# Moving two kinds of low-part subtraction from VectorE, which read PSUM, to GpSimd, which reads an SBUF copy made by ScalarE

## The chip, the cores and the metric

The kernel runs on one core of a Trainium2 chip. The metric is the device time of one execution in microseconds. Engines are named as in the profile: PE is TensorE (matmuls; PEld its weight loads), DVE is VectorE, ACT is ScalarE, POOL is GpSimd, SP is the engine whose queue issues most of the DMAs.

## The reference, cut to what matters

Attention that keeps the 32 largest scores of each row, then a feed-forward layer with a gated activation, then a layer of eight experts of which each token uses one. All inputs are float32.

```python
scores = scale * np.matmul(q, k.transpose(0, 1, 3, 2))   # 4 batches, 8 heads, 576 rows, 64 wide
kth = np.partition(scores, -32, axis=-1)[..., -32:-31]
scores = np.where(scores >= kth, scores, -1e9)
...
x = np.matmul(softmax(scores), v)                         # heads joined: 2304 tokens x 512
h = x @ w_in                                              # 512 -> 2048
g = h * np.clip(h + 3.0, 0.0, 6.0) / 6.0
x = g @ w_out                                             # 2048 -> 512
...
ye = np.maximum(x[mask] @ w1[e], 0.0) @ w2[e]             # 8 experts, mask = tokens of expert e
out[mask] = gate_w[mask, None] * ye
```

## The kernel before, in words

**High and low parts.** TensorE multiplies in a rounded float32 format here. An operand is therefore kept as a rounded part (h) and the remainder that rounding dropped (l), and a product is built from two or three matmuls. A remainder is made by a subtraction: unrounded value minus rounded value. For the transposed queries the parts are `qh` and `ql`, for the transposed attention output `xh` and `xl`.

**Tiles and visits.** The 576 query rows of a batch are cut where blocks of 256 tokens end, so parts are 64, 128, 192 or 256 rows wide. A visit (48 in all, numbered n) is one part of one pair of heads. A visit holds one tile per head and 128 rows, and for the last 64 rows one tile "T" that stacks both heads: 144 tiles t in all. At a change of batch the visits of the old and the new batch alternate, and visits 64 rows wide hold one tile only.

**The loop over tiles.** Step t of the main loop puts work of several tiles side by side: the score matmuls of tile t+2 (`qk`, L585, into `sps`), their copy to SBUF by ACT (`sevac`, into `sbuf`), the search for the largest scores on DVE (`top_a`: L615, L621, L626; `top_z`: L648; `mask`: L675, L679, L683), the transposes of the probabilities (`trans`, L699, into `ptps`), the product with v (`pv`, L733), and one step g of the feed-forward layer (`moe_step`: L807 into `l1ps`, L819 on DVE, `gh` and `gl` on POOL, L838 into `yps`). In the first 34 steps or so each step also converts one piece of the feed-forward weights (`conv64`: L293, L300, L303 on DVE, L262 and L311 on POOL).

**Preparing queries.** `qprep(n)` transposes the rows of visit n on PE (L434, and L436 for a last 64 rows) into the single-buffer PSUM tile `misc`; ACT copies it with rounding to `qh` (L442, L448); DVE subtracts `qh` from the PSUM tile into `ql` (L452, L456). Both are read by the score matmuls of that visit. The raw rows come by DMA into the tile `qn` (L488, L491, on SP's queue), which has one buffer: the DMAs of visit n+1 wait until the transposes of visit n have read it. Keys are prepared alike by `kprep` (L402, L403 on POOL, L409, L417 on PE).

**Turning the attention output.** `xt` transposes the output of 128 rows and two heads on PE (L769) into `misc`; ACT copies with rounding to `xh` (L779); DVE subtracts into `xl` (L783). Both are operands of L807. It runs 80 times, 16 of them for a tile T, where both ACT and DVE work in two pieces of 64x64.

**What sets the order.** Each engine works in order. A scheduler sets that order at build time from priorities (the table `PRIO`) and its own estimate of when things are ready, so a change of one instruction can move its neighbours.

After the attention loop, from about 860 us on, the rest of the feed-forward layer and the experts follow.

Of the kernel before, what the change touches and what calls it, by code (L numbers as in the profile page):

```python
# [13 lines left out]
F32 = mybir.dt.float32  # L14
# [4 lines left out]
AF = mybir.ActivationFunctionType  # L19
ALU = mybir.AluOpType  # L20
# [36 lines left out]
def attention_two_moe_kernel(  # L57
# [13 lines left out]
    PE, V, A, G, SP = nc.tensor, nc.vector, nc.scalar, nc.gpsimd, nc.sync  # L71
# [4 lines left out]
    NE, _, F2 = w1.shape  # L76
    P = 128
# [53 lines left out]
    def r_(ap):  # L131
        return ap.bitcast(F32)
# [4 lines left out]
    def pr(name, least=0):  # L137
        tc.cur_priority = max(least, pr0[0] + PRIO[name])

    def run(gen):  # L140
        for _ in gen:
            pass
# [54 lines left out]
    def body(cs, exact):  # L197
# [12 lines left out]
        ap1 = at.enter_context(tc.tile_pool(name="ap1" + X, bufs=1, side="right"))  # L210
# [20 lines left out]
        def misc(shape):  # L231
            m = boot.pop(0) if boot else None
            if m is not None:
                return m if len(shape) == 3 else m[:, 0:shape[1]]
            misc_n[0] += 1
            return ps1.tile(shape, F32, tag="misc", bufs=1, name=f"misc{misc_n[0]}")
# [147 lines left out]
        def rows(h):  # L384
            return slice(h * D, (h + 1) * D)
# [40 lines left out]
        def qprep(n):  # L426
            b, p, q0, w, first = visits[n]
            pr(pk[0])
            qn = qraw.pop(n)
            nf = w // P  # L430
            mp = misc([P, 2, 2 * P])
            for h in range(2):
                for j in range(nf):
                    PE.transpose(mp[:, h, j * P:(j + 1) * P], qn[:, j, h, :, :].rearrange("p a d -> p (a d)"), ident)  # L434
                if w % P:
                    PE.transpose(mp[:, h, nf * P:w], qn[0:TAIL, nf, h, :, :].rearrange("p a d -> p (a d)"), ident[0:TAIL, 0:TAIL])  # L436
            yield
            pr(pk[0])
            fw = nf * P
            st = [ap1.tile([P, 2, 2 * P], F32R, tag=f"q{i}", bufs=QB, name=f"q{i}{n}") for i in "hl"]  # L440
            if nf:
                A.activation(st[0][:, :, 0:fw], mp[:, :, 0:fw], AF.Copy)  # L442
            if w % P:

                for i in st:
                    G.memset(r_(i[:, :, fw:fw + P]), 0.0)  # L446
                for h in range(2):
                    A.activation(st[0][:, h, fw + h * D:fw + (h + 1) * D], mp[:, h, fw:w], AF.Copy)  # L448
            yield
            pr(pk[0])  # L450
            if nf:
                V.tensor_tensor(st[1][:, :, 0:fw], mp[:, :, 0:fw], r_(st[0][:, :, 0:fw]), op=ALU.subtract)  # L452
            if w % P:
                for h in range(2):
                    hc = slice(fw + h * D, fw + (h + 1) * D)
                    V.tensor_tensor(st[1][:, h, hc], mp[:, h, fw:w], r_(st[0][:, h, hc]), op=ALU.subtract)  # L456
            qx[n] = st
            yield
            pr(pk[0])
# [73 lines left out]
        def pstart(tl, age=AGE):  # L533
            if pjob[0] is None:
                kind = pick(tl, age)
                if kind == "k":
                    pjob[0] = ("k", kprep(*kjobs[kdone[0]]))
                elif kind == "q":
                    pjob[0] = ("q", qprep(qdone[0]))
            return pjob[0]  # L540
# [219 lines left out]
        def xt(n, o, t):  # L760
            b, p, q0, w, first = visits[n]
            r0 = b * S + q0
            bk, off = divmod(r0, TB)
            xh, xl = xbuf[bk % 2]
            while bk >= 2 and gpos[0] < (bk - 1) * NF1:
                run(moe_step())
            mp = misc([P, P])
            pr("xt0")
            PE.transpose(mp, xp.pop((n, o)), ident)  # L769
            yield  # L770
            if o == "T":
                off += w // P * P
                parts = [(rows(h), slice(off, off + 64), rows(h)) for h in range(2)]
            else:
                off += o * P
                parts = [(slice(0, P), slice(off, off + P), slice(0, P))]
            pr("xt1")
            for r, cl, m in parts:
                A.activation(xh[r, p, cl], mp[r, m], AF.Copy)  # L779
            yield  # L780
            pr("xt2")
            for r, cl, m in parts:
                V.tensor_tensor(xl[r, p, cl], mp[r, m], r_(xh[r, p, cl]), op=ALU.subtract)  # L783
            if t == vlast[n] and p == NPAIR - 1 and (r0 + w) % TB == 0:
                blkready[0] = bk + 1

# [177 lines left out]
        def moe_step():  # L964
            g = gpos[0]
            if g >= NG + 3 or (g < NG and blkready[0] <= g // NF1):
                return
            gpos[0] += 1
            if 0 <= g - 1 < NG:
                epi_a(g - 1)  # L970
            yield
            if g >= 3:
                l2(g - 3)
                bk, f = divmod(g - 3, NF1)
                if f == NF1 - 1:
                    for tt, y in enumerate(yevac(bk)):
                        pend.append([gate(bk, tt, y), 0])
            yield
            if 0 <= g - 1 < NF1:
                conv_upto(2 * (g - 1) + 1)  # L980
            if 0 <= g - 1 < NG:
                load_wo(g - 1)
            if 0 <= g - 2 < NG:
                epi_c(g - 2)
            yield
            if 0 <= g - 1 < NG:
                epi_b(g - 1)
            yield
            if g < NG:
                if g < NF1:  # L990
                    conv_upto(2 * g)
                l1(g)
# [29 lines left out]
        for t in range(T + 7):  # L1022
# [23 lines left out]
            if xtq and (xtq[0][2] < t - 5 or t >= T):  # L1046
                xg = xt(*xtq.pop(0))
                next(xg)
# [141 lines left out]
        for s in range(len(seq) + 2):  # L1190
            if s < len(seq):
                e, f = seq[s]
# [85 lines left out]
    with tc.If(todo > 0):  # L1278
# [4 lines left out]
        for e in range(NE):  # L1283
            n = nc.values_load(ctl[0:1, 2 + e:3 + e], min_val=0, max_val=NT)
# [32 lines left out]
```

## Time and profile before

| what | value |
|---|---|
| median of 3 runs | 1261.87 us (1261.56 to 1262.14) |
| profiled execution, its own time | 1263.75 us |
| its span, first to last instruction | 1261.9 us |
| busy over the span: PE, DVE, ACT, POOL | 91%, 76%, 65%, 32% |
| mean granted TensorE clock | 0.968 |

The busy shares are averages over stages with different limits: DVE is 7 to 9 tenths busy in every slice from 32 us to about 850 us and mostly 2 to 4 tenths after that. The profiled execution took 1263.75 us, 1.88 us above the median, and 1.85 us of it lie around the span.

### The profile page before, as it was taken

Reading aid. Unit: us, or ns where it says so; the run is one execution under the profiler, and the core shown is the slowest. Engines: PE = TensorE matmul, PEld = TensorE weight load, DVE = VectorE, ACT = ScalarE, POOL = GpSimd, SP = SyncE. Lnnn points to the kernel's source line nnn. Section 1 sums busy time; section 2 is a strip of 40 time slices with the busy share of each in tenths; the row PEclk is TensorE's granted clock in tenths of the full one; section 3 lists DMA queues with packets and bytes.
Section 4 is the critical chain, followed back from the end, with each engine's and each line's share of the span. In section 5 each row is a group of like instructions: output and inputs, shape, how many; then the busy total and the mean of one; then the engine's idle time right before and its main releaser. Section 6 shows DMA issues by size and latency. Waiting matters only on the chain.

```text
span 1261.9 us, 23710 instructions
## 1 busy us (share of the span) xinstructions
PE 1146.6 (91%) x7333; PEld 1031.2 (82%) x7333; DVE 954.9 (76%) x3820; ACT 816.7 (65%) x2089; POOL 408.1 (32%) x649
## 2 busy tenths in 40 slices
PE   5476579899999999999999999999985999999995
PEld 4365467789999899999898999998875999999994
DVE  5999999999999899998997999995413444444420
ACT  4777777778888788787777887784413444444421
POOL 3542255743322443323433322223433022221100
PEclk9998689999999999999999999999986999999997
DMA  3644456555543555634435545444854455455400
GB/s 89 207 131 141 127 173 228 151 163 144 143 136 123 133 153 154 163 117 132 123 107 156 144 121 148 124 120 123 305 174 118 150 179 156 155 174 154 128 19 26
DMA packets 184664, 180.20 MB, mean 143 GB/s; under 512 B 123933, under 2 KB 148813, under 8 KB 184528
## 3 DMA queue, kind: packets, MB, share of 16 engines
q1 hardware_dynamic: 178960, 167.24, 45.5%
q0 software_dynamic: 4416, 11.08, 2.9%
q8 instruction: 60, 0.98, 0.3%
q14 instruction: 76, 0.62, 0.2%
q10 hardware_dynamic: 1152, 0.28, 0.1%
HBM read 160.52 MB, written 19.59 MB: 143 GB/s over the span
## 4 chain that ended last, share of the span: by engine, by line
PE 69%; DVE 18%; ACT 5%; DMA 4%; issue 2%; POOL 1%; SPq 0%; POOLq 0%; DVEq 0%; ACTq 0%
PE l1ps L807 12%; PE yps L838 12%; PE lp L1152 11%; PE ops L1169 10%; PE ptps L733 8%; PE sps L585 5%; PE ptps L699 4%; DVE pbuf L683 3%; DVE z L648 2%; DVE cd L615 2%; DVE z L675 2%; DVE cw L626 1%; DVE m L621 1%; PE misc L434 1%; PE misc L409 1%
## 5 line engine op out<-in xcount | busy, mean ns | idle before, releaser
L838 PE MATMUL yps<-wo,gh 128*128 128x512 f32 x576 | 217.4, 419 | 0.5 <-DMA wo<-wod 0.5
L615 DVE MAX8 cd<-sbuf 128x8 f32<-128x72 f32 x1152 | 187.2, 218 | 2.8 <-ACT sbuf L264 2.5
L262 POOL TENSOR_SCALAR gh<-gf 128x256 fp32r<-128x256 f32 x144 | 73.7, 512 | 355.4 <-PE yps L838 233.9
L807 PE MATMUL l1ps<-xh,wih 128*128 128x256 f32 x576 | 168.8, 293 | 14.3 <-DVE gf L819 7.0
L807 PE MATMUL l1ps<-xl,wih 128*128 128x256 f32 x576 | 165.2, 287 | 0.0
L807 PE MATMUL l1ps<-xh,wil 128*128 128x256 f32 x576 | 164.6, 286 | 0.0
L956 DVE TENSOR_TENSOR wl<-raw,wh 128x1024 fp32r<-128x1024 f32 x64 | 79.2, 1239 | 94.8 <-ACT wh L955 92.7
L733 PE MATMUL ptps<-vn,pt 128*128 128x65 f32 (+1 forms) x1152 | 146.5, 281 | 0.0
L733 PEld LDWEIGHTS ptps<-vn,pt 128*128 128x128 f32 x1152 | 143.5, 201 | 0.0
L683 DVE SCALAR_TENSOR_TENSOR pbuf<-sbuf,tall,pbuf 128x576 f32<-128x576 f32 x144 | 135.2, 939 | 0.1
L648 DVE SCALAR_TENSOR_TENSOR z<-sbuf,uall 128x576 f32<-128x576 f32 x144 | 131.2, 911 | 2.5 <-ACT uall L639 2.4
L807 PEld LDWEIGHTS l1ps<-xh,wih 128*128 128x128 f32 x576 | 111.0, 193 | 24.7 <-DVE gf L819 11.9
L955 ACT ACTIVATE wh<-raw 128x1024 fp32r<-128x1024 f32 x64 | 67.6, 1060 | 84.0 <-PE lp L1152 44.7
L838 PEld LDWEIGHTS yps<-wo,gh 128*128 128x128 f32 x576 | 108.0, 191 | 16.9 <-POOL qh L446 0.7
L827 POOL TENSOR_TENSOR gl<-gf,gh 128x256 fp32r<-128x256 f32 x144 | 118.1, 820 | 11.3
L838 PE MATMUL yps<-wo,gl 128*128 128x512 f32 x288 | 116.5, 405 | 0.6 <-POOL gl L827 0.6
L699 PE MATMUL ptps<-ident,pbuf 128*128 128x128 f32 x576 | 97.9, 295 | 20.0 <-DVE j L679 17.4
L807 PEld LDWEIGHTS l1ps<-xl,wih 128*128 128x128 f32 x576 | 111.4, 193 | 4.3
L665 ACT ACTIVATE jk<-sbuf,uall 128x576 bf16<-128x576 f32 x144 | 112.0, 777 | 4.3 <-DVE j L679 0.8
L264 ACT ACTIVATE sbuf<-sps 128x576 f32<-128x576 f32 x144 | 93.1, 647 | 32.3 <-PE sps L585 21.5
L656 ACT ACTIVATE pbuf<-sbuf,nb 128x576 f32<-128x576 f32 x144 | 111.3, 776 | 4.1 <-PE ptps L701 0.8
L807 PEld LDWEIGHTS l1ps<-xh,wil 128*128 128x128 f32 x576 | 111.5, 194 | 0.0
(197 smaller groups left out, 2934.5 us busy)
## 6 DMA issues: line engine op xcount, KB each, us to landing
wo<-wod SPq DMA_DIRECT2D x144, 512.0 KB, 3.8
raw<-in_moe_w_dram SPq DMA_DIRECT2D x64, 512.0 KB, 4.0
vn<-in_v_dram SPq DMA_DIRECT2D x96, 128.0 KB, 2.7
rawi<-in_moe_w_in_dram SPq DMA_DIRECT2D x16, 512.0 KB, 4.1
rawo<-in_moe_w_out_dram SPq DMA_DIRECT2D x16, 512.0 KB, 3.8
wod<-wc SPq DMA_DIRECT2D x16, 512.0 KB, 3.8
qn<-in_q_dram SPq DMA_DIRECT2D x126, 64.0 KB, 2.6
yd<-y SPq DMA_DIRECT2D x18, 258.0 KB, 4.1
```

The costliest lines, as they stand in the source:

```text
L615: V.max(cd[:, c, :], s[:, c * CK:(c + 1) * CK])
L648: V.scalar_tensor_tensor(d["z"], s, d["u"], s, op0=ALU.is_le, op1=ALU.mult)
L656: A.activation(d["p"], d["s"], AF.Exp, bias=d["nb"], scale=SCALE)
L665: A.activation(jk, d["s"][:, 0:S], AF.Sign, bias=ts[t]["u"], scale=-1.0, accum_out=d["sg"])
L683: V.scalar_tensor_tensor(d["p"], d["s"], tall[:, t:t + 1], d["p"], op0=ALU.is_ge, op1=ALU.mult)
L699: PE.transpose(ptps[:, c * P:(c + 1) * P], pb[:, c0 + c * P:c0 + (c + 1) * P], ident)
L733: PE.matmul(d_, a_, b_, start=(i == 0), stop=(i == len(mm) - 1))
L807: PE.matmul(dst, a[:, c, fs], b_[:, c, :], start=(n == 0), stop=(n == 3 * NCC - 1))
L827: G.tensor_tensor(gl, gf, r_(gh), op=ALU.subtract)
L838: PE.matmul(yps[tt], a[:, tsl], b_, start=(f == 0 and m == 0), stop=(f == NF1 - 1 and m == 2))
L1152: PE.matmul(lp, a[:, c, fs], b_[:, c, :], start=(n == 0), stop=(n == 3 * NCC - 1))
L1169: PE.matmul(ops_[j], a[:, js], b_[:, ns], start=(f == 0 and m == 0), stop=(f == NF2 - 1 and m == 2))
```

## The change

`qprep`, for every visit but the first, has ACT copy the PSUM tile a second time, unrounded, into a new SBUF tile `qr`; POOL subtracts `qh` from `qr` into `ql`. The tile `qr` uses the one buffer of the tag `qn`, the raw query rows. `xt` has ACT copy its PSUM tile unrounded into a new SBUF tile `xr` (two buffers of its own); POOL subtracts `xh` from it into `xl`.

```diff
             pr(pk[0])
+            if n == 0:
+                e_, qr = V, mp
+            else:
+                e_, qr = G, ap1.tile([P, 2, 2 * P], F32, tag="qn", bufs=1, name=f"qr{n}")
+                A.activation(qr[:, :, 0:w], mp[:, :, 0:w], AF.Copy)
             if nf:
-                V.tensor_tensor(st[1][:, :, 0:fw], mp[:, :, 0:fw], r_(st[0][:, :, 0:fw]), op=ALU.subtract)
+                e_.tensor_tensor(st[1][:, :, 0:fw], qr[:, :, 0:fw], r_(st[0][:, :, 0:fw]), op=ALU.subtract)
             if w % P:
                 for h in range(2):
                     hc = slice(fw + h * D, fw + (h + 1) * D)
-                    V.tensor_tensor(st[1][:, h, hc], mp[:, h, fw:w], r_(st[0][:, h, hc]), op=ALU.subtract)
+                    e_.tensor_tensor(st[1][:, h, hc], qr[:, h, fw:w], r_(st[0][:, h, hc]), op=ALU.subtract)
...
             for r, cl, m in parts:
                 A.activation(xh[r, p, cl], mp[r, m], AF.Copy)
+            xr = ap1.tile([P, P], F32, tag="xr", bufs=2, name=f"xr{n}_{o}")
+            A.activation(xr, mp, AF.Copy)
             yield
             pr("xt2")
             for r, cl, m in parts:
-                V.tensor_tensor(xl[r, p, cl], mp[r, m], r_(xh[r, p, cl]), op=ALU.subtract)
+                G.tensor_tensor(xl[r, p, cl], xr[r, m], r_(xh[r, p, cl]), op=ALU.subtract)
```

In the rows below a name carries the visit or tile number and then a buffer number; lines of the changed kernel are 5 to 7 higher than those of before.

On DVE before, at visit 4 in the weight-conversion stage (z, j8 and pbuf belong to the tiles in work, cvi to a weight piece):

```order
L303 SCALAR_TENSOR_TENSOR cvi5_1020<-rawi5_822,cvi5_1020 128x512
L675 MAX z8_9_1011<-z9_975 128x8
L648 SCALAR_TENSOR_TENSOR z10_1033<-sbuf0_141,uall_160 128x576
L679 SCALAR_TENSOR_TENSOR j8_9_1012,tall_159<-ptps_126,sg9_938,z8_9_1011 128x16
L452 TENSOR_TENSOR ql4_1074<-misc17_1068,qh4_1073 128x512
L683 SCALAR_TENSOR_TENSOR pbuf1_139<-sbuf4_145,tall_159,pbuf1_139 128x576
```

And on DVE in the changed kernel, the same place:

```order
L303 SCALAR_TENSOR_TENSOR cvi5_1032<-rawi5_828,cvi5_1032 128x512
L626 MAX m8_11_1011<-cw11_1013 128x8
L680 MAX z8_9_1023<-z9_985 128x8
L653 SCALAR_TENSOR_TENSOR z10_1045<-sbuf0_141,uall_160 128x576
L684 SCALAR_TENSOR_TENSOR j8_9_1024,tall_159<-ptps_126,sg9_948,z8_9_1023 128x16
L620 MAX cd12_1089<-sbuf2_143 128x8
L688 SCALAR_TENSOR_TENSOR pbuf1_139<-sbuf4_145,tall_159,pbuf1_139 128x576
```

The subtraction into ql4 is gone between the match (L679, now L684) and the mask (L683, now L688); one piece of the next tile's search stands there.

On POOL in the changed kernel, the same stretch (wih, wil, wc are the weight parts):

```order
L790 TENSOR_TENSOR xl0_134<-xr1_0_1006,xh0_133 128x128
L262 TENSOR_SCALAR wih_130<-cvi5_1032 128x4x128
L311 TENSOR_TENSOR wil_131<-cvi5_1032,wih_130 128x4x128
L457 TENSOR_TENSOR ql4_1086<-qr4_1123,qh4_1085 128x512
L262 TENSOR_SCALAR wc5_1117<-cvo5_1109 128x512
L311 TENSOR_TENSOR wc5_1117<-cvo5_1109,wc5_1117 128x512
L790 TENSOR_TENSOR xl0_134<-xr1_1_1151,xh0_133 128x128
```

Before, the four weight instructions followed each other with nothing between them; now three subtractions stand around and among them.

On POOL in the changed kernel at a change of batch (visits 39 and 40; gh and gl are parts of the feed-forward layer):

```order
L834 TENSOR_TENSOR gl86_10572<-gf86_10374,gh86_10571 128x256
L461 TENSOR_TENSOR ql39_10412<-qr39_10417,qh39_10411 128x64 x2
L694 MEMSET pbuf2_140 64x64
L262 TENSOR_SCALAR gh87_10671<-gf87_10510 128x256
L834 TENSOR_TENSOR gl87_10672<-gf87_10510,gh87_10671 128x256
L457 TENSOR_TENSOR ql40_10527<-qr40_10529,qh40_10526 128x512
L790 TENSOR_TENSOR xl0_134<-xr35_0_10558,xh0_133 128x128
```

ql39 stands behind gl86 and ql40 behind gh87 and gl87, where before both were DVE's.

## Rows read from the trace of the kernel before

**Rows 1.** Stretch, length; busy us of PE, PEld, DVE, ACT, POOL; clock; DMA share, GB/s.

```profile
14.00:220.00 206.00, 143.54 (x720) 120.95 (x721) 199.67 (x743) 153.31 (x393) 86.61 (x104) 0.90 0.52 161
220.00:345.00 125.00, 120.39 (x863) 106.89 (x862) 120.08 (x544) 99.80 (x296) 57.78 (x105) 1.00 0.55 152
345.00:600.00 255.00, 252.83 (x1872) 235.06 (x1871) 239.26 (x1118) 203.77 (x568) 86.06 (x134) 1.00 0.51 140
```

**Rows 2.** Chain that ended last, shares by line: 14:220, 220:345, 345:600 us.

```profile
by line: DVE pbuf L683 11.0%; DVE cd L615 8.3%; DVE z L648 7.7%; DVE z L675 7.0%; issue 6.7%; DVE cvi L303 4.1%; PE sps L585 4.0%; DVE cw L626 3.8%; DVE m L621 3.8%; PE ptps L733 3.6%; DVE cvo L303 2.9%; DVE cvi L300 2.9%; DVE cvi L293 2.4%
by line: PE l1ps L807 10.3%; PE yps L838 10.1%; DVE z L648 6.8%; PE ptps L733 6.3%; DVE pbuf L683 6.1%; DVE cd L615 5.8%; PE ptps L699 4.6%; PE sps L585 4.5%; DVE z L675 4.2%; DVE m L621 3.0%; DVE cw L626 2.9%; ACT pt L264 2.6%; PE misc L43
by line: PE l1ps L807 25.0%; PE yps L838 24.8%; PE ptps L733 17.3%; PE sps L585 9.4%; PE ptps L699 8.0%; PE misc L434 1.8%; PE ptps L866 1.7%; DMA kd<-in_k_dram 1.5%; PE misc L409 1.5%; PE misc L858 1.1%; PE misc L769 1.1%; PE ptps L701 1.0
```

**Rows 3.** DVE instructions that read misc (L452, L456, L783), by stretch.

```profile
14.00:220.00 206.00, 8.64 (x21) 0.90 0.52 161
220.00:345.00 125.00, 10.29 (x41) 1.00 0.55 152
345.00:600.00 255.00, 16.08 (x45) 1.00 0.51 140
600.00:710.00 110.00, 8.70 (x34) 1.00 0.47 122
710.00:900.00 190.00, 9.53 (x26) 1.00 0.51 152
```

**Rows 4.** Waits of DVE from 14 to 220 us: total, times, longest.

```profile
DVE z L648 <- ACT uall L639: 2.4, 3, 1.3
DVE ql L452 <- ACT qh L442: 1.8, 2, 1.0
DVE xl L783 <- ACT xh L779: 0.3, 1, 0.3
```

**Rows 5.** Instructions by shape: busy us, mean ns of one, idle before.

```profile
L442 ACT ACTIVATE qh<-misc 128x512 fp32r<-128x512 f32 x23 | 13.6, 593 | 3.3 <-PE misc L434 3.1
L779 ACT ACTIVATE xh<-misc 128x128 fp32r<-128x128 f32 x64 | 17.6, 276 | 5.1 <-PE misc L769 4.4
...
L452 DVE TENSOR_TENSOR ql<-misc,qh 128x512 fp32r<-128x512 f32 x23 | 15.7, 682 | 2.0 <-ACT qh L442 1.8
```

**Rows 6.** POOL subtractions: ns min/median/max, first and last start, shape.

```profile
L403 POOL TENSOR_TENSOR kd<-kd x15: 1265/1285/1884, 17.5 to 670.8; 128x512 fp32r<-128x512 f32 x15
L827 POOL TENSOR_TENSOR gl<-gf,gh x144: 725/741/1697, 168.2 to 944.5; 128x256 fp32r<-128x256 f32 x144
L403 POOL TENSOR_TENSOR ke<-ke x15: 447/453/933, 12.7 to 672.4; 64x128 fp32r<-64x128 f32 x15
```

**Rows 7.** Timeline around 131.5 us: start, duration, instruction.

```profile
131.55 1.26 POOL L311 TENSOR_TENSOR wc<-cvo,wc 128x512 fp32r<-128x512 f32 x1
131.66 1.77 DVE L648 SCALAR_TENSOR_TENSOR z<-sbuf,uall 128x576 f32<-128x576 f32 x1
```

**Rows 8.** The two mask lines: all of L648 (min/median/max), then groups in 14:220.

```profile
L648 DVE SCALAR_TENSOR_TENSOR z<-sbuf,uall x144: 790/802/1851, 18.3 to 863.1; 128x576 f32<-128x576 f32 x144
L648 DVE SCALAR_TENSOR_TENSOR z<-sbuf,uall 128x576 f32<-128x576 f32 x29 | 33.9, 1169 | 2.4 <-ACT uall L639 2.4
L683 DVE SCALAR_TENSOR_TENSOR pbuf<-sbuf,tall,pbuf 128x576 f32<-128x576 f32 x28 | 28.7, 1026 | 0.0
```

**Rows 9.** Timeline at a change of batch, 678 to 683 us.

```profile
678.67 0.34 PE L436 MATMUL misc<-ident,qn 64*128 64x64 f32 x2
679.03 1.92 SPq L488 DMA_DIRECT2D qn<-in_q_dram  x4
679.42 0.32 ACT L448 ACTIVATE qh<-misc 128x64 fp32r<-128x64 f32 x2
680.18 0.34 DVE L456 TENSOR_TENSOR ql<-misc,qh 128x64 fp32r<-128x64 f32 x2
682.00 0.92 PE L434 MATMUL misc<-ident,qn 128*128 128x128 f32 x4
```

## The prediction, made before the changed kernel ran

> **What bounds the kernel now.** The shares of busy time mislead here, so I read by stretch, first the busy time and then, for the same stretches, the chain of work that ended last. From 14 to 220 us, while the weights are converted, DVE is busy 199.67 of 206 us and PE 143.54 [rows 1]; the chain is mostly DVE's own lines, search, masks and conversion [rows 2]. Time taken off DVE there should come off the end almost one for one. From 220 to 345 us both are nearly full (DVE 120.08, PE 120.39 of 125) and the chain changes between them: the DVE lines shown add up to 6.8 + 6.1 + 5.8 + 4.2 + 3.0 + 2.9 = 28.8%. From 345 to 600 us PE is busy 252.83 of 255 us, and no DVE line reaches 1% of the chain; DVE is busy 239 us there but nobody waits for it in the end. From 600 us to the end of attention it is between these two. So the same removed microsecond is worth about 1 early, 0.3 in the second stretch and almost nothing later.
>
> **What leaves DVE.** The instructions that read `misc` on DVE are just the moved ones: 8.64 us of them from 14 to 220 us, 10.29 to 345 us, 16.08 to 600 us, 8.70 and 9.53 after that [rows 3]; the first visit's stays. Early, their waits for ACT's rounded copy leave too: 1.8 and 0.3 us [rows 4]. That is 8.6 + 2.1 = 10.7 us in the first stretch, if nothing else takes these gaps. In the second it is 10.3 x 0.288 = 3.0 us. For the later 34.3 us the shares are about 1% at best in one stretch and under 28.8% in the others; I take 7% on average of the 18.2 us after 600 us and 1% of the rest, 1.3 + 0.2 = 1.5 us.
>
> **What ACT gains.** A second copy of the same shape has the price of the first: 593 ns for 512 columns and 276 for 128 [rows 5]. From 14 to 220 us there are 7 query copies, 1 small one and 12 of 128 columns (21 moved subtractions, the small visit has two): 7 x 0.593 + 13 x 0.276 = 7.7 us on an engine busy 153 of 206 us. It has room, but DVE waits for ACT a little in order: 2.4 us for `uall` [rows 4]. Bounds: 0, and 7.7 us if each copy stood in DVE's way; I take 1.0, since DVE's waits for ACT are few. Later some 37 us of copies come (23 of 512 columns, 16 of 256 to 384, 8 of 128 and 80 of `xr` are about 45 in all). The one ACT line that shows in the chain of the second stretch has 2.6%; at 5% for all of ACT that is 1.9 us.
>
> **What POOL gains, and what that does to DVE.** The least time of a subtraction on POOL is 1265 ns for 512 columns, 725 for 256 and about 447 for 128 [rows 6]; 64 columns I estimate at 320 by the same slope. That is 7 x 1.265 + 12 x 0.447 + 2 x 0.32 = 14.9 us early and about 90 us in all (23 x 1.265 + 16 x 0.725 + 64 x 0.447 + 64 x 0.32), so some 75 us later. POOL was busy 87 of 206 us, so its own time is covered. But at 131.66 us the mask product L648, which takes 802 ns as a rule, took 1.77 us: POOL's L311 had begun 0.11 us before and ran for 1.26 [rows 7, 8]. The DVE instruction stood still until POOL had done. In the first stretch L648 and L683 together lost 33.9 + 28.7 - (29 + 28) x 0.802 = 16.9 us beside 86.6 us of POOL work, that is 0.19 us for each microsecond of POOL. The added 14.9 us cost 2.9 us by that rate (bounds 0 and 14.9). Over the later stretches such losses count by DVE's small share of the chain: 75 x 0.19 = 14 us at most, a tenth of it at the weights above, less where POOL's instructions are shorter; I take 0.6.
>
> The Trainium skill speaks against this change in the same place: its page "SBUF — State Buffer", section "SBUF: two separate sides", says that a VectorE instruction with two SBUF inputs and a GpSimd instruction that reads SBUF use one shared port pair, that whichever starts first holds it for its whole duration, and that the other blocks fully. By that rule, the trace agrees in the pair of rows just quoted. The subtractions that leave DVE had PSUM as one input, so by the rule they did not take part; those that come to POOL do. By the rule alone, with every new subtraction paid in full by DVE, the first stretch would lose 14.9 us and not 2.9.
>
> **What is queued behind the new waits.** The raw rows of the next visit, and now `qr` of this one, share one buffer. Before, the next DMA went out when the transposes had read it: at 679.03 us, right after L436 at 678.67, and its rows were transposed at 682.00 [rows 9]. That visit had been just in time. Now the DMA must wait for ACT's rounded copies (end 679.74), the unrounded copy (0.276) and two subtractions on POOL (0.64), that is until 680.7 at the earliest: 1.7 us later, with the DMAs behind it on SP's queue, while PE has the transposes next in its order. In the changed order `ql39` also stands behind `gl86` on POOL, and `ql40` behind `gl87`. The next visit's own `ql` comes 0.593 + 1.265 - 0.682 = 1.2 us later as well [rows 5, 6], so such a place costs between 0 (PE finds other work) and 2.9 us. With 256 rows a visit lasts four tiles and a late load is covered by the visit in work; the visits of one tile at the two changes of batch that have them (about 222 and 620 to 690 us) have no such cover. I count two places at 1.7 us, 3.4 us.
>
> **The sum.** First stretch: -10.7 + 2.9 + 1.0 = -6.8 us. Later: -3.0 - 1.5 + 0.6 + 1.9 + 3.4 = +1.4 us. Together -5.4 us. The profiled execution took 1263.75 us, so the changed kernel's should take about 1258.4; against the median, 1.88 us lower, 1261.87 - 5.4 = 1256.5 us.
>
> **Rivals.**
> - *More stays.* The late loads are covered everywhere, and the second stretch, where DVE and PE both wait, gains more than the chain's share. Without the 3.4 us the result is 1253; if half of the 10.3 us counts in place of 3.0, 1251. For it: PE's 120 busy us in 125 leave a gap that DVE partly makes. Against it: PE's own work is then the floor. Chance 0.16.
> - *It is given back and nothing is left.* The early wait moves: DVE, freed of a subtraction, waits for ACT's `uall` or `pt` in its place, so that the pace of a step stays. Then the change does not do what it says in its one useful stretch: about 1261.9 + 0 to 1, within 0.2%. For it: ACT's order is what DVE's waits name [rows 4]. Against it: these waits are 2.4 us of 206, so DVE is the one that is late. Chance 0.22, with the milder cases of the next two.
> - *Late loads at many visits.* Fourteen visits lie in the two alternating runs that hold one-tile visits. Each that is just in time costs up to 2.9 us on PE. The gain without such places is 5.4 + 3.4 = 8.8 us; at 4 places of 2.3 us it is gone, from 5 or 6 on the kernel is slower by over 0.2%, at 8 it takes 1261.87 - 8.8 + 18.4 = 1271. For it: the rows around 679 us. Against it: at the other changes the load of the next visit has more time. Chance 0.10.
> - *POOL holds DVE.* If the new subtractions fall on the masks as L311 did on L648 at 131.66 us, each costs DVE its whole duration: 14.9 in place of 2.9 us early, 12 us more, 1268.5. It decides from about 8.3 us of early blocking on, where the sum is zero, against 2.9. The Trainium skill's rule on the shared port pair, named above, makes the blocking possible; how often it strikes is not in it. Against it: POOL's long conversions follow DVE's by a fixed beat, the new ones come at all phases. Chance 0.08.
>
> **How the numbers follow.** A measurement of this kernel can tell about 0.2%, 2.5 us. The forecast's own case, 1254 to 1259.3, has 0.44; with the first rival faster has 0.60, the same 0.22, slower 0.18. The range reaches down to 1249, the case that more stays with the blocking at its lower bound, and up to 1266, between the two slower cases, which leaves out about 2 in 10.
>
> **What would show it.** Right: the stretch to the end of the weight conversion shorter by 6 to 7 us with DVE still over 95% busy in it; L648 and L683 longer on average by some 0.05 us there; ACT's total up by 45 us and POOL's by 90 to 105, DVE's down by some 43; a wait of SP's q loads for POOL's subtraction in place of PE's transposes. Wrong: if DVE shows new waits for ACT in the first stretch; if the masks' mean time rises past 1.3 us there; if PE waits for `ql` or for q rows by more than 3 us at the changes of batch; or if 345 to 600 us, which is PE's, changes its length.

## The result, and the profile after

The changed kernel took 1273.06 us (median of 4 runs, 1272.93 to 1276.43), the kernel before beside it 1261.71: a ratio of 1.0101, 95% interval 1.0079 to 1.0123. It is slower by about 12.8 us (0.0101 x 1262), where 5.4 us less were forecast. Its profiled execution has a span of 1274.6 us, 12.7 more than before.

The same stretches after (stretch, length; busy us of PE, PEld, DVE, ACT, POOL; clock; DMA share, GB/s), to set against [rows 1]:

```profile
14.00:220.00 206.00, 136.90 (x720) 116.22 (x721) 199.28 (x722) 157.12 (x412) 108.93 (x125) 0.88 0.52 161
220.00:345.00 125.00, 115.96 (x811) 102.58 (x810) 109.59 (x486) 98.80 (x306) 72.76 (x137) 0.97 0.51 144
345.00:600.00 255.00, 251.21 (x1850) 233.76 (x1849) 237.61 (x1087) 214.36 (x611) 117.24 (x178) 1.00 0.49 139
```

In the second stretch PE is busy 116.0 us in place of 120.4 and DVE 109.6 in place of 120.1: neither is the bound there any more, both wait. The chain of that stretch shows for whom. GpSimd's lines, of which [rows 2] shows none among the largest for before, are in it now:

```profile
by line: PE yps L845 10.3%; PE l1ps L814 9.0%; PE ptps L738 7.4%; issue 7.2%; PE sps L590 6.7%; DVE z L653 5.1%; PE ptps L704 4.3%; DVE cd L620 3.9%; POOL kd L403 3.1%; DMA kd<-in_k_dram 3.0%; POOL gl L834 2.8%; DVE pbuf L688 2.7%; DVE z L6
```

**Where the time is lost.** The mask instruction on DVE comes once for each tile, so its start is a mileage mark. Timeline of before (start, duration, instruction), the 25th, 33rd, 109th and last of its 144:

```profile
198.16 0.81 DVE L683 SCALAR_TENSOR_TENSOR pbuf<-sbuf,tall,pbuf 128x576 f32<-128x576 f32 x1
252.91 0.80 DVE L683 SCALAR_TENSOR_TENSOR pbuf<-sbuf,tall,pbuf 128x576 f32<-128x576 f32 x1
682.52 0.81 DVE L683 SCALAR_TENSOR_TENSOR pbuf<-sbuf,tall,pbuf 128x576 f32<-128x576 f32 x1
869.90 0.82 DVE L683 SCALAR_TENSOR_TENSOR pbuf<-sbuf,tall,pbuf 128x576 f32<-128x576 f32 x1
```

The same four in the changed kernel:

```profile
196.86 0.80 DVE L688 SCALAR_TENSOR_TENSOR pbuf<-sbuf,tall,pbuf 128x576 f32<-128x576 f32 x1
256.91 0.82 DVE L688 SCALAR_TENSOR_TENSOR pbuf<-sbuf,tall,pbuf 128x576 f32<-128x576 f32 x1
696.86 0.80 DVE L688 SCALAR_TENSOR_TENSOR pbuf<-sbuf,tall,pbuf 128x576 f32<-128x576 f32 x1
880.26 0.82 DVE L688 SCALAR_TENSOR_TENSOR pbuf<-sbuf,tall,pbuf 128x576 f32<-128x576 f32 x1
```

It is 1.3 us ahead at the 25th tile, 4.0 behind at the 33rd, 14.3 behind at the 109th and 10.4 behind at the last. Between the 97th (7.0 behind) and the 109th it loses another 7.3 us, but there the mark itself swings: the kernel below that moves the attention output alone goes from 2.4 us ahead to 3.8 behind at the same tiles and ends attention 3.4 ahead. The remaining 2.3 us of the span's 12.7 come after attention; they were not followed up. So there are two questions: why the first stretch gained 1.3 us and not 6.8, and what costs 5.3 us in the eight tiles behind it.

**The first stretch.** The DVE instructions with two SBUF inputs, from 14 to 220 us (busy us, mean ns, idle before). First the conversion lines of before, then all six groups after; the masks of before are in [rows 8]:

```profile
L303 DVE SCALAR_TENSOR_TENSOR cvi<-rawi,cvi 128x512 uint32<-128x512 uint32 x15 | 10.2, 678 | 0.0
L300 DVE SCALAR_TENSOR_TENSOR cvi<-rawi,cvi 128x512 uint32<-128x512 uint32 x15 | 10.1, 671 | 0.0
L303 DVE SCALAR_TENSOR_TENSOR cvo<-rawo,cvo 128x512 uint32<-128x512 uint32 x14 | 9.5, 679 | 0.0
L300 DVE SCALAR_TENSOR_TENSOR cvo<-rawo,cvo 128x512 uint32<-128x512 uint32 x14 | 9.4, 671 | 0.0
```

```profile
L653 DVE SCALAR_TENSOR_TENSOR z<-sbuf,uall 128x576 f32<-128x576 f32 x29 | 34.2, 1178 | 3.4 <-ACT uall L644 3.4
L688 DVE SCALAR_TENSOR_TENSOR pbuf<-sbuf,tall,pbuf 128x576 f32<-128x576 f32 x28 | 30.4, 1085 | 0.0
L300 DVE SCALAR_TENSOR_TENSOR cvo<-rawo,cvo 128x512 uint32<-128x512 uint32 x14 | 12.0, 856 | 0.0
L300 DVE SCALAR_TENSOR_TENSOR cvi<-rawi,cvi 128x512 uint32<-128x512 uint32 x15 | 11.6, 770 | 0.0
L303 DVE SCALAR_TENSOR_TENSOR cvo<-rawo,cvo 128x512 uint32<-128x512 uint32 x14 | 10.6, 758 | 0.0
L303 DVE SCALAR_TENSOR_TENSOR cvi<-rawi,cvi 128x512 uint32<-128x512 uint32 x15 | 10.4, 691 | 0.0
```

Together 101.8 us before (33.9 + 28.7 + 39.2) and 109.2 after, in the same counts: 7.4 us more, against 8.64 us of subtractions that left [rows 3]. That is 1.2 us of gain, and the mark shows 1.3. So close a match is partly luck: the kernel below that moves the narrow visits alone, with one small visit in this stretch, has the same mark 1.95 us ahead. The idle time did not fall either: it is 206 - 199.67 = 6.3 us before and 6.7 after. In place of the waits that left with the subtractions [rows 4] others grew, as DVE's waits from 14 to 220 us show (total, times, longest; the first line is before, the others after):

```profile
DVE j L679 <- ACT jk L665: 1.3, 1, 1.3
DVE z L653 <- ACT uall L644: 3.4, 3, 2.2
DVE j L684 <- ACT jk L670: 1.7, 1, 1.7
DVE cvo L293 <- DMA rawo<-in_moe_w_out_dram: 1.1, 1, 1.1
```

The wait for `uall` grew by 1.0 us [rows 4] and that for `jk` by 0.4; the wait for a DMA of raw weights is new, and so is one of 0.4 us for ACT's `pt`.

**The change of batch.** The timeline of POOL in the changed kernel at visit 10, which has 192 rows. ACT's copy L455 for it runs from 230.79 to 231.29 us:

```profile
230.71 1.12 POOL L402 TENSOR_SCALAR kd<-kd 128x512 fp32r<-128x512 f32 x1
231.91 1.27 POOL L403 TENSOR_TENSOR kd<-kd 128x512 fp32r<-128x512 f32 x1
233.15 0.29 POOL L402 TENSOR_SCALAR ke<-ke 64x128 fp32r<-64x128 f32 x1
233.53 0.93 POOL L403 TENSOR_TENSOR ke<-ke 64x128 fp32r<-64x128 f32 x1
234.40 0.30 POOL L446 MEMSET qh<- 128x256 f32 x1
234.68 0.40 POOL L262 TENSOR_SCALAR gh<-gf 128x256 fp32r<-128x256 f32 x1
235.16 0.72 POOL L834 TENSOR_TENSOR gl<-gf,gh 128x256 fp32r<-128x256 f32 x1
235.84 0.72 POOL L457 TENSOR_TENSOR ql<-qr,qh 128x256 fp32r<-128x256 f32 x1
```

The inputs of the subtraction were ready at 231.3 and it started at 235.84, behind seven instructions, most of them of the key preparation and the feed-forward layer. Visit 10 is the only one of the 24 visits of under 256 rows where it began more than 1 us after its copy had ended; at 18 of them it began within 0.5 us. Elsewhere, then, it is the copy and POOL's longer operation that make the remainder late, more than POOL's queue. On DVE before, the same remainder was made at 230.90 us:

```profile
230.90 0.42 DVE L452 TENSOR_TENSOR ql<-misc,qh 128x256 fp32r<-128x256 f32 x1
```

PE stood still for it in the changed kernel (timeline of PE; in brackets the idle time before it and what ended it):

```profile
236.62 0.61 PE L590 MATMUL sps<-kx,ql 128*128 128x288 f32 x1 [2.83 <-POOL ql L457]
```

And a second loss follows the first, as the windows of 2 us there show (columns as above; the clock is the third number from the end):

```profile
232.00:234.00 2.00, 1.29 (x9) 0.84 (x8) 2.00 (x8) 0.00 (x0) 1.92 (x3) 1.00 0.80 261
234.00:236.00 2.00, 0.00 (x0) 0.00 (x0) 2.00 (x18) 0.00 (x0) 1.92 (x5) 0.80 0.01 3
236.00:238.00 2.00, 1.38 (x6) 1.37 (x7) 0.98 (x3) 0.26 (x1) 1.30 (x3) 0.50 0.00 0
238.00:240.00 2.00, 2.00 (x11) 2.00 (x11) 0.00 (x0) 1.97 (x6) 0.00 (x0) 0.50 0.15 33
240.00:242.00 2.00, 2.00 (x9) 1.90 (x8) 1.12 (x6) 0.85 (x3) 0.00 (x0) 0.50 0.73 111
242.00:244.00 2.00, 2.00 (x14) 1.52 (x13) 0.64 (x5) 1.38 (x5) 0.46 (x1) 0.99 0.72 151
```

PE did nothing from 233.79 to 236.62 us, and its granted clock fell from full speed to half, the 1.2 GHz level, and stayed there until 242 us. In the chain twelve matmuls of the feed-forward layer took this long (start, us; after at the half clock, then before at full clock):

```profile
237.92 2.56 PE l1ps L814 x12
234.06 1.44 PE l1ps L807 x12
```

At half the clock, PE lost about 0.5 x (242 - 236.62) = 2.7 us in which it had work. Meanwhile ACT and DVE ran out of work. The Trainium skill, "TensorE: Matmul & The Clock Gate", section "HAM oscillation — how this bites in real kernels", describes this chain: a wait lets the clock fall, and the next work starts cold. This trace agrees, at a wait of 2.83 us.

From 220 to 885 us PE's waits for the two lines of the moved subtraction are 11.4 us in 13 (total, times, longest):

```profile
PE sps L590 <- POOL ql L457: 8.8, 9, 2.8
...
PE sps L590 <- POOL ql L461: 2.6, 4, 1.0
```

Ten of these waits, 7.8 us, are at visits of under 256 rows, and three, 3.6 us, at visits of 256 rows. Before, there was one such wait:

```profile
PE sps L585 <- DVE ql L456: 1.1, 1, 1.1
```

All waits of PE listed for that stretch add up to 10.6 us before and 19.9 after, so the late remainder covers the whole increase of its listed waits.

### The profile page after: what moved, and what is told of

The parts are those of the page before. It is cut to its first block, busy times and chain, and to the rows that moved or that the text cites. A ratio compares the mean times of both kernels' runs of the same rounds, so it can differ in the third digit from the quotient of the medians.

```text
span 1274.6 us, 23911 instructions
## 1 busy us (share of the span) xinstructions
PE 1143.8 (90%) x7333; PEld 1031.5 (81%) x7333; DVE 935.4 (73%) x3653; ACT 840.4 (66%) x2216; POOL 520.4 (41%) x816
## 4 chain that ended last, share of the span: by engine, by line
PE 63%; DVE 18%; ACT 5%; POOL 5%; issue 4%; DMA 4%; SPq 0%; POOLq 0%; ACTq 0%; DVEq 0%
PE yps L845 11%; PE l1ps L814 11%; PE lp L1159 11%; PE ops L1176 10%; PE ptps L738 7%; PE sps L590 4%; PE ptps L704 3%; DVE cd L620 3%; DVE z L653 3%; DVE pbuf L688 3%; DVE z L680 2%; DVE m L626 1%; DVE cw L631 1%; PE tp L1141 1%; POOL kd L403 1%
## 5 line engine op out<-in xcount | busy, mean ns | idle before, releaser
L620 DVE MAX8 cd<-sbuf 128x8 f32<-128x72 f32 x1152 | 184.6, 217 | 12.9 <-ACT sbuf L264 12.7
L738 PE MATMUL ptps<-vn,pt 128*128 128x65 f32 (+1 forms) x1152 | 143.3, 278 | 0.0
L688 DVE SCALAR_TENSOR_TENSOR pbuf<-sbuf,tall,pbuf 128x576 f32<-128x576 f32 x144 | 140.9, 979 | 0.5
L653 DVE SCALAR_TENSOR_TENSOR z<-sbuf,uall 128x576 f32<-128x576 f32 x144 | 136.1, 945 | 6.4 <-ACT uall L644 6.0
L738 PEld LDWEIGHTS ptps<-vn,pt 128*128 128x128 f32 x1152 | 140.4, 198 | 0.0
L834 POOL TENSOR_TENSOR gl<-gf,gh 128x256 fp32r<-128x256 f32 x144 | 128.9, 895 | 10.9
L704 PE MATMUL ptps<-ident,pbuf 128*128 128x128 f32 x576 | 98.6, 295 | 15.8 <-DVE j L684 15.3
```

The costliest lines, as they stand in the source:

```text
L620: V.max(cd[:, c, :], s[:, c * CK:(c + 1) * CK])
L653: V.scalar_tensor_tensor(d["z"], s, d["u"], s, op0=ALU.is_le, op1=ALU.mult)
L688: V.scalar_tensor_tensor(d["p"], d["s"], tall[:, t:t + 1], d["p"], op0=ALU.is_ge, op1=ALU.mult)
L704: PE.transpose(ptps[:, c * P:(c + 1) * P], pb[:, c0 + c * P:c0 + (c + 1) * P], ident)
L738: PE.matmul(d_, a_, b_, start=(i == 0), stop=(i == len(mm) - 1))
L834: G.tensor_tensor(gl, gf, r_(gh), op=ALU.subtract)
```

## The experiments

Two theories stood at the start. A: the query remainder comes late (a second ACT copy, a longer operation on POOL, POOL's queue), and PE feels it where a visit lasts one or two tiles. B: POOL's added time holds DVE, or POOL's other work, wherever it falls. Of the 47 moved visits 23 have 256 rows (wide), 24 have 64 to 192 (narrow); the narrow ones lie around the changes of batch. Every ratio is to runs of the kernel before on the same chip, whose medians were 1263.6 to 1263.9 us in these comparisons; 0.001 is 1.26 us.

**The two parts apart.** First only the query remainders move, then only those of the attention output; the other part is as before.

```diff
 e1_ql_alone
-            xr = ap1.tile([P, P], F32, tag="xr", bufs=2, name=f"xr{n}_{o}")
-            A.activation(xr, mp, AF.Copy)
...
-                G.tensor_tensor(xl[r, p, cl], xr[r, m], r_(xh[r, p, cl]), op=ALU.subtract)
+                V.tensor_tensor(xl[r, p, cl], mp[r, m], r_(xh[r, p, cl]), op=ALU.subtract)
 e2_xl_alone
-            if n == 0:
+            if True:
                 e_, qr = V, mp
```

> Only the query remainders move to GpSimd; those of the attention output stay on VectorE. If the loss is made by ql coming late at the changes of batch, nearly all of the 11 us stays: 1270 to 1274, with PE waiting 10 us or more for POOL's ql. If it is made by the port (VectorE's two-input instructions standing still behind GpSimd), the loss goes with GpSimd's added time, of which this has some 60 of 100 us: 1267 to 1269, spread over the run. If ACT's extra copies make it, this has half of them: about 1267.

> Only the remainders of the attention output move; the queries stay on VectorE. Late ql as the cause: 1259 to 1263, no step in the lag at the changes of batch. Port as the cause: 40 of 100 us of the added GpSimd time, 1264 to 1267. ACT's copies as the cause: 1266 to 1267. If the in-order queue of GpSimd, blocked by xl waiting for ACT, is what holds other work, PE waits for gl or kd here and it is above 1265.

Measured: 1283.68 us, 1.0151 (1.0128 to 1.0175), and 1260.5 us, 0.9974 (0.9963 to 0.9984). The query remainders alone lose more than the whole change, and more than any range named for them; the attention output's are a gain of 3.3 us. Added up, the parts give 1.0125, which agrees with the 1.0101 of the whole within the intervals. The clock takes part: in windows of 10 us, the first kernel's profiled run is below full clock in eight stretches after 200 us, the whole change's in two, before's in one (0.95). Three of the eight, columns as above:

```profile
260.00:270.00 10.00, 10.00 (x58) 8.55 (x58) 8.46 (x39) 6.40 (x19) 5.45 (x13) 0.83 0.71 211
500.00:510.00 10.00, 8.37 (x44) 7.15 (x43) 5.94 (x19) 5.34 (x18) 5.44 (x7) 0.79 0.43 93
510.00:520.00 10.00, 10.00 (x67) 9.39 (x66) 8.52 (x47) 7.59 (x20) 2.79 (x4) 0.87 0.50 154
```

**A buffer of its own for the copy of narrow visits**, so that the next raw rows need not wait for POOL; two small constants share one buffer to make the room.

```diff
-                e_, qr = G, ap1.tile([P, 2, 2 * P], F32, tag="qn", bufs=1, name=f"qr{n}")
+                e_, qr = G, ap1.tile([P, 2, 2 * P], F32, tag="qn", bufs=1, name=f"qr{n}") if w == 2 * P else ap1.tile([P, 2, 3 * D], F32, tag="qr", bufs=1, name=f"qr{n}")
```

> As the run that moves the query remainders alone, but for visits of 64 to 192 rows the unrounded copy has a buffer of its own, so that the rows of the next visit load as early as before the change (two constants share a buffer to make room). If the late load is the cause, most of the loss of that run goes: 1260 to 1264. If the late ql itself is (ACT's second copy, then GpSimd's queue), it stays within 2 us of that run.

Measured: 1282.8 us, 1.0157 (1.013 to 1.0184), no change from 1.0151. With the remainder late (PE still waits for POOL's `ql` in this trace, 3.27 us at the longest), an earlier load of rows gains nothing. The prediction's mechanism, the late load, is not what this kernel loses its time to.

**The copies alone.** ACT makes both unrounded copies, nobody reads them, and DVE subtracts from PSUM as before. Then only the copies of the queries, and only those of narrow visits.

```diff
-                e_, qr = G, ap1.tile([P, 2, 2 * P], F32, tag="qn", bufs=1, name=f"qr{n}")
+                e_, qr = V, ap1.tile([P, 2, 2 * P], F32, tag="qn", bufs=1, name=f"qr{n}")
                 A.activation(qr[:, :, 0:w], mp[:, :, 0:w], AF.Copy)
+                qr = mp
...
-                G.tensor_tensor(xl[r, p, cl], xr[r, m], r_(xh[r, p, cl]), op=ALU.subtract)
+                V.tensor_tensor(xl[r, p, cl], mp[r, m], r_(xh[r, p, cl]), op=ALU.subtract)
```

The second and third leave out the copy into `xr`; the third has `n == 0 or w == 2 * P` in place of `n == 0`.

> Both unrounded copies are made by ACT, the one of queries in the shared buffer, but nobody reads them: VectorE subtracts from PSUM as before. If ACT's load or the load of q rows that waits for the copy is the cause: 1267 or more. If late ql or the port is: 1262 to 1265.

> ScalarE's unrounded copies of the queries alone, read by nobody; all subtractions on VectorE from PSUM, nothing new on GpSimd. The copies of both kinds gave 1.0053. If the copies of the queries are what cost there: 1268 to 1271. If the 80 small copies of the attention output: 1263 to 1265. The loss with GpSimd's unread subtractions added was 1.0105, so what is between that and this run is what GpSimd's time costs by itself.

> ScalarE's unrounded copies of the queries of narrow visits alone, read by nobody; nothing new on GpSimd. Between this and the kernel that adds GpSimd's unread subtraction (1.0085) lies what GpSimd's work and the later release of the buffer cost. Theory L or G: 1264 to 1266. If ScalarE's copies delay the rounded ones and the rest of its queue: 1270 or more.

Measured: 1269.9 us, 1.0053 (1.0032 to 1.0073); 1267.35, 1.0031 (1.002 to 1.0042); 1264.92, 1.0004 (0.9992 to 1.0016). ACT's copies are not free: all of them cost 6.7 us where nobody gains by them, but those of narrow visits cost nothing that can be measured. By difference the copies of wide visits cost 0.0027, 3.4 us. The copies of queries also hold the buffer of the next raw rows longer, and no run separates that from ACT's time. The second run lies between the two ranges named for it.

**By the width of the visit.**

```diff
 e5_wide_ql and e7_narrow_ql: attention output on VectorE, as before, and
-            if n == 0:
+            if n == 0 or w < 2 * P:      # e7_narrow_ql: n == 0 or w == 2 * P
                 e_, qr = V, mp
```

> Only the query remainders of 256-row visits go through the ScalarE copy and GpSimd; narrower visits and all remainders of the attention output stay on VectorE. Moving all query remainders alone took 20 us more than before. Theory A (the query remainder itself comes late, and is felt where a visit lasts one or two tiles, at the changes of batch): most of the 20 us goes, 1264 to 1268. Theory B (VectorE is held by GpSimd over their common port, wherever a subtraction falls): the loss goes with GpSimd's time, and as 30 of the 47 moved visits stay moved and have the longest subtractions, 1276 to 1280.

> The counterpart: only the query remainders of visits of under 256 rows move. Theory A: it keeps most of the 20 us, 1276 to 1283. Theory B: 1264 to 1268, as these subtractions are short. If both halves lose about 10 us each, neither the width of the visit nor the port decides, but each late remainder on its own.

Measured: 1270.2 us, 1.0042 (1.0021 to 1.0063), and 1279.09, 1.0121 (1.0104 to 1.0137). The count in the first expectation was wrong: 23 visits stay moved, not 30. The narrow visits, with the shorter subtractions, hold 15.3 us and the wide ones 5.3; the two halves add up to about the whole (0.0042 + 0.0121 against 0.0151). Theory A has most of it, but the wide visits' 5.3 us are more than it gave them. In the profiled run of the wide kernel (1271.18 us) this loss is hardly a late remainder: PE's waits for `ql` made by POOL are 1.1 us from 220 to 885 us, and the mark falls from 2.6 to 8.1 us behind between the 103rd and the 104th tile, where the clock drops (columns as above):

```profile
640.00:650.00 10.00, 8.45 (x53) 6.75 (x52) 9.16 (x36) 8.10 (x25) 2.65 (x11) 0.91 0.47 131
650.00:660.00 10.00, 10.00 (x49) 9.60 (x49) 4.44 (x23) 3.56 (x9) 1.50 (x4) 0.57 0.19 59
```

Just before, PE had waited 1.09 us for ACT's `y`, a piece of the feed-forward output, and 0.46 us for DVE's match `j`. Whether the other executions, 1265.52 to 1275.95 us, have this drop is not on record.

**The copy one step earlier**, ahead of the rounded copies.

```diff
             st = [ap1.tile([P, 2, 2 * P], F32R, tag=f"q{i}", bufs=QB, name=f"q{i}{n}") for i in "hl"]
+            if n == 0:
+                e_, qr = V, mp
+            else:
+                e_, qr = G, ap1.tile([P, 2, 2 * P], F32, tag="qn", bufs=1, name=f"qr{n}")
+                A.activation(qr[:, :, 0:w], mp[:, :, 0:w], AF.Copy)
...
```

> As the kernel that moves the query remainders alone (1283.7), but ScalarE makes the unrounded copy one step earlier, before the rounded ones. Theory A, if ScalarE's place in the chain is what makes the remainder late: 1270 to 1276. Theory A, if GpSimd's longer operation and its queue make it late: 1281 to 1286, no gain, since the rounded copy then comes 0.6 us later and the subtraction is issued in the same step. Theory B: no change, 1281 to 1286.

Measured: 1284.9 us, 1.0167 (1.015 to 1.0184). Nothing gained. In its trace the copy of visit 10 ends 0.7 us after the transposes and POOL's subtraction still begins 5.4 us after them: at this visit its place in POOL's queue decides, not the copy.

**Shadows: POOL works, but nobody waits for it.** DVE makes the remainder that PE reads, as before; ACT's copy and POOL's subtraction are made over the copy and left unread. First for all 47 visits, then for the narrow ones, then for these with the buffer of their own as above.

```diff
-                e_.tensor_tensor(st[1][:, :, 0:fw], qr[:, :, 0:fw], r_(st[0][:, :, 0:fw]), op=ALU.subtract)
+                V.tensor_tensor(st[1][:, :, 0:fw], mp[:, :, 0:fw], r_(st[0][:, :, 0:fw]), op=ALU.subtract)
+                if n:                                # e11, e13: if w < 2 * P
+                    G.tensor_tensor(qr[:, :, 0:fw], qr[:, :, 0:fw], r_(st[0][:, :, 0:fw]), op=ALU.subtract)
...
```

> As the kernel that moves the query remainders alone (1283.7), but VectorE makes the remainder that TensorE reads, from PSUM as before; ScalarE's copy and GpSimd's subtraction are still made, with the result written over the copy and read by nobody. Theory A (TensorE waits for a late query remainder): the loss goes, up to ScalarE's extra copies, 1263 to 1270. Theory B (GpSimd's new work holds VectorE, or delays GpSimd's other work): 1280 or more, since VectorE has its subtraction back and all of the rest stays.

> As the kernel that moves only the query remainders of narrow visits (1279.1, with 11.4 us of waits of TensorE for them), but VectorE makes the remainder that TensorE reads, from PSUM as before; ScalarE's copy and GpSimd's subtraction are made all the same, over the copy, and read by nobody. Theory A (TensorE waits for a late remainder, and its clock falls behind the wait): 1264 to 1270. Theory B (GpSimd's added work delays what else GpSimd and VectorE do at these visits): 1275 to 1281, since that work is all still there.

> As the narrow visits' unread subtraction (1.0085), but ScalarE's copy has a buffer of its own, so that the next raw rows go out as before, and TensorE should no longer wait for rows of q (2.3 us in five waits there). Theory L (the late load is what is left, hidden behind the late remainder where that is late as well): 1264 to 1268. Theory G (GpSimd's added work at these visits delays its other work and VectorE): 1272 to 1276, no change.

Measured: 1277.94 us, 1.0105 (1.0083 to 1.0127); 1273.96, 1.0085 (1.0068 to 1.0101); 1269.04, 1.0039 (1.0027 to 1.0052). All three lie between the ranges of their two theories, so neither theory explains one by itself. Theory A as it stood falls: with no late remainder at all, two thirds of the loss stay. In the narrow shadow PE waits for rows of q, for which the list of the kernel before has no row (waits of PE):

```profile
PE misc L434 <- DMA qn<-in_q_dram: 1.6, 3, 0.8
PE misc L436 <- DMA qn<-in_q_dram: 0.6, 2, 0.5
```

and what holds their DMAs on SP's queue is POOL's subtraction:

```profile
SPq L500 <- POOL qr L465: 8.8, 3, 5.8
SPq L497 <- POOL qr L465: 6.9, 5, 3.3
```

With the own buffer these waits are gone, and 0.0046 of the ratio with them. For the narrow visits this makes a ladder: ACT's copies +0.0004 (0.5 us), POOL's unread work +0.0035 (4.4), the later load +0.0046 (5.8), the late remainder itself +0.0036 (4.5), together 0.0121. Two steps change more than one thing: the copies alone were made in the shared buffer and the next rung has a buffer of its own, and in the last step DVE's own subtraction goes as well. Each step is uncertain by about 0.002, each kernel got its order anew from the scheduler, and the ladder holds in this order only: taken off first, as above, the later load gives nothing.

**Put together: the attention output and some of the queries.**

```diff
 e9_xl_wide: only the attention output, and of it only 256-row visits
+            e_, xr = V, mp
+            if w == 2 * P:
+                e_, xr = G, ap1.tile([P, P], F32, tag="xr", bufs=2, name=f"xr{n}_{o}")
+                A.activation(xr, mp, AF.Copy)
...
 e10_all_xl_wide_ql: the whole change, but
-            if n == 0:
+            if n == 0 or w < 2 * P:
                 e_, qr = V, mp
 e14_xl_and_first_ql: the whole change, but
-            if n == 0:
+            if n == 0 or n > 7:
                 e_, qr = V, mp
```

> Only remainders of the attention output move, and of these only those of 256-row visits; the query remainders and those of narrower visits stay on VectorE. All remainders of the attention output moved gave 0.9974 of before. Theory A (what is moved costs where visits are narrow and gains elsewhere): better still, 1256 to 1259. Theory B (each moved subtraction gains or loses by itself, wherever it is): 64 of some 80 moves are left or fewer, so 0.998 to 0.999, 1261 to 1262.

> The whole change, but the query remainders of visits of under 256 rows stay on VectorE. The parts alone were 1.0042 (wide query remainders) and 0.9974 (attention output). Theory A (late remainders of narrow visits): most of the loss of 11 us goes, 1262 to 1267. Theory B (GpSimd's time as such, through the common port or its queue): it keeps 70% of the added GpSimd time, 1268 to 1272.

> All remainders of the attention output move, and of the query remainders only those of visits 1 to 7, which are made before 220 us, where the forecast had its gain. If the first stretch keeps what it gains there (mask of tile 24 at 196.6 us in the kernel that has both, 197.9 with the attention output alone): 1257 to 1260, 1 to 2 us under the kernel that moves the attention output alone (0.9974). If that gain is not carried to the end, because the stretch behind it is TensorE's: 1260 to 1262.

Measured: 1262.13 us, 0.9985 (0.997 to 1.0); 1264.02, 1.0009 (1.0 to 1.0019); 1262.62, 0.9983 (0.9971 to 0.9994). The second takes all but 1.1 us of the whole change's loss away by leaving 24 visits where they were. The first shows no harm done by narrow visits to the attention output's part: with 48 of its 80 copies left (not 64, as the expectation had it) about half of the gain is left, though its interval reaches 1.0. The third has its 25th mask at 195.64 us, 1.5 us ahead of the kernel that moves the attention output alone (197.09), and still does not end earlier: what the first stretch gains there is not carried to the end. The best version stays the one that moves the attention output's remainders alone, 0.9974, faster than the kernels before and after; by their intervals the first and the third cannot be told from it.

## Why the prediction was wrong

**The step that failed most** is "I count two places at 1.7 us, 3.4 us". It looked at the late load and at visits of one tile at two changes of batch. Measured, the narrow visits cost the whole change 0.0101 - 0.0009 = 0.0092, 11.6 us, uncertain by some 3 us. The number of places was wrong: there are 24 narrow visits, and PE waits at them ten times. The mechanism was wrong in part: the prediction saw that `ql` would come 1.2 us later by ACT's copy and POOL's longer operation, but counted a place at the 1.7 us of the load alone, and it saw `ql39` and `ql40` behind a `gl` in POOL's order without asking how long that queue is when a key preparation stands in it. At visit 10 it is 4.5 us. And nothing in the sum allowed for the clock, which lost about 2.7 us behind the wait at visit 10. All that comes after the first stretch was put at +1.4 us and came out at some +14 between the profiled runs (12.7 + 1.3). One more term of it was too small: ACT's copies, at 1.0 + 1.9 us, cost 6.7 us when made alone, with the later release of the buffer in it.

**The first stretch**, -10.7 + 2.9 + 1.0 = -6.8, came out at -1.3. Of -10.7 the 8.6 us of instructions left as said; the 2.1 us of waits did not, since the waits for `uall`, `jk`, `pt` and raw weights grew by 2.9 us. Against the 2.9 us of blocking the two-input lines grew by 7.4: the rate was taken from L648 and L683 alone, while L300 and L303 have two SBUF inputs as well and took 5.4 of the 7.4 us, the masks 2.0. POOL's busy time rose by 22.3 us and not 14.9. The rule that the prediction weighed, of the Trainium skill, "SBUF — State Buffer", section "SBUF: two separate sides", names any VectorE instruction with two SBUF inputs; the trace agrees in that these four groups grew. But POOL's new work is not shown to be all of it: in the kernel with both of ACT's copies and nothing new on POOL, the masks of this stretch took 34.6 + 30.7 = 65.3 us, 2.7 more than before, and the conversion lines L300 and L303 averaged 698 ns in place of 676, some 1.3 us over all 58. So about 4 of the 7.4 us appear without it, perhaps from a new phase between the two engines, and what POOL's work adds may be no more than the 2.9 us forecast. How much is open.

**The second stretch.** "10.3 x 0.288 = 3.0 us" of gain presumed that the bound stays where it was. With PE waiting for POOL, DVE's time there can have been worth little: DVE is idle 15.4 of 125 us after.

**What came as said.** The prices were near: POOL's subtraction of 512 columns took 1382 ns on average (1265 forecast, the least time of its like), ACT's copy of 512 columns 604 (593 forecast):

```profile
L457 POOL TENSOR_TENSOR ql<-qr,qh 128x512 fp32r<-128x512 f32 x23 | 31.8, 1382 | 30.8 <-ACT qr L455 23.7 <-DVE cd L620 2.6 <-ACT nb L641 2.5
L455 ACT ACTIVATE qr<-misc 128x512 f32<-128x512 f32 x23 | 13.9, 604 | 0.0
```

The copies add 45.7 us of durations on ACT (45 forecast), though ACT's busy time rose by 23.7 us only, as the durations of its neighbouring instructions overlap; POOL's busy time rose by 112 us (90 to 105). DVE's total fell by 19.5 us and not 43: its two-input lines took some 15 us back over the span, and the rest was not followed up. SP's q loads wait for POOL's subtraction, 28.1 us in 14 waits at L457, as said. The sign that was named for a wrong prediction, waits of PE for `ql` of more than 3 us, is there with 11.4 us. So are new waits of DVE for ACT in the first stretch.

**The rivals.** *Late loads at many visits* (1271) came nearest in time, and its places were right; the late load it rests on costs 5.8 us only when the remainder is on time. *POOL holds DVE* was to decide from 8.3 us of early blocking on; 7.4 at most were found, which takes the gain but makes no loss. *Given back* describes the first stretch. None had the query remainder waiting in POOL's queue.

**Open.** What POOL's unread work at narrow visits delays (4.4 us): in the narrow shadow a `gl` that started at 234.99 us before starts at 236.48, behind the two new subtractions, but that PE loses its time by such delays was not tested. Open is also the 4.4 us that the wide visits' query remainders cost beside the attention output's (1.0009 - 0.9974 = 0.0035): their copies alone cost 0.0027, so POOL may have little part in it.

## What to carry to other kernels

Before an instruction moves to another engine's queue, read from the trace what that queue holds at the tightest consumer, not on average: POOL was busy 32% of the span, and at one visit without slack a remainder still stood 4.5 us behind seven instructions, which cost a wait of 2.83 us and then the clock. Count too what the detour itself needs: here a second copy, a longer operation, and an input buffer that is held longer, which cost 5.8 us where the remainder was on time. Split a move by how much slack its consumer has: the attention output's remainder, for which PE waits 0.3 us in the whole changed kernel, went to POOL with a gain of 3.3 us; moving the query remainders of narrow visits with it lost 11.6. When costing blocking between two engines, list every instruction that has the operands for it, not the one group that showed it.

## What the runs showed of the hardware

In the changed kernel the granted clock fell to half within a wait of PE of 2.83 us and stayed there for some 6 us more, where PE had work. In the kernel that moves the query remainders of wide visits it fell behind waits of 1.09 and 0.46 us, and the windows from 640 to 660 us show 0.91 and 0.57. The executions of the kernel that moves the query remainders alone spread from 1281.44 to 1288.64 us; its profiled one, of span 1286.9, has 8 stretches of 10 us below full clock, while that of the kernel with the copy's own buffer, of span 1281.6 and nearly the same median, has 3. That the price of such waits differs between executions of one program would explain the spread, but of each program one execution has a trace, so it is not shown.
